# A gated feed-forward layer on one core: ten sums change from GpSimd to VectorE, and one unit more divides its S3 T3 product

## The chip, the cores and the metric

The kernel runs on one core of a Trainium2 chip. A core has a matrix engine (TensorE; PE in the profile, PEld for its weight loads), a vector engine (VectorE, DVE), an engine for functions (ScalarE, ACT), a general one (GpSimd, POOL), and a queue that starts DMAs (SyncE, SP). Each engine works through its own list of instructions in order and waits where one needs a result of another engine. The metric is the device time of one execution in microseconds; lower is better.

## The reference

The layer has 2048 tokens of width 1024 and an inner width of 3584, all in bfloat16:

```python
g = jnp.einsum("bsd,df->bsf", x, w_gate)      # 2048 x 1024 times 1024 x 3584
u = jnp.einsum("bsd,df->bsf", x, w_up)
h = gelu(g) * u                               # tanh form
return jnp.einsum("bsf,fd->bsd", h, w_down)   # 2048 x 3584 times 3584 x 1024
```

## The kernel before

**Products by seven instead of eight.** The kernel multiplies matrices as 2 x 2 blocks with Winograd's scheme: seven block products and some sums in place of eight products. On the weights' side the sums are called S1 to S4, on the side of x they are T1 to T4; a block that is only copied to another type is sa or tb. The sums are float32, so their matmuls read 128x512 float32 tiles.

**Tiling.** Tokens are worked in two passes p of 1024, each pass in two halves of 512 columns. The inner width is cut into 14 units of 256 columns (NU = 14), two blocks of 128 each, for w_gate and w_up (i = 0, 1). A block product (product) takes KH = 4 matmuls of 128x512, one per 128 rows of a half of K. For a unit and a pass the seven products are P1 (raw weights), S and G (raw, second half of K, for passes 0 and 1), P6 (S2 T2), P5 (S1 T1), and S4 Tb, SA T4 and S3 T3.

**Three stages.** First the units 0 to 2, one pass at a time (unit, over the list items; the last item is unit 0, pass 1). Then the joint units 3 to 13 (JOINT = 3), which take both passes together. Then the down projection (down).

**The second division.** In the joint units a product for gate and up and for both passes is itself a 2 x 2 block matrix: rows are gate and up, the inner index is the two halves of four K blocks, columns are the two passes. inner cuts it again by the same scheme: seven half products of two matmuls each, 14 matmuls, in place of four whole products of four, 16. Its left sums are quarter sums of S (half_sums, split_sums, on POOL); its right sums go over both passes. For these, split_b makes for each k of 0 and 1, from blocks b11, b12, b21 and b22 (rows: halves of K, columns: passes), n1 = b12 - b11, n2 = b22 - n1 and n4 = b21 - n2; split_b_rest makes n3 = b22 - b12 in place of b12, and so must come after everything that reads b12 as it was. The products named X (S4 Tb) and K (SA T4) are divided in all joint units. H (S3 T3) is divided from unit DIVIDED7 = 5 on; in units 3 and 4, H2, H3 and H4 are the whole products and the other H names do nothing.

**Where the T sums are made.** Those of Tb: split_b("tb") on POOL in the first stage, the rest in the last item's p4 (line 1117). Those of T4: there as well, split_b("t4") ahead of whole_p4 and split_b_rest("t4") behind it, all on POOL (pool, line 108). Some results go to a tile named w that more_room takes from the weights' pool. Those of T3: split_b3 in three parts, part 0 (three sums) at the end of unit DIVIDED7 - 1 (at @t4.1), parts 1 and 2 (three and two) in unit DIVIDED7 (at @s3), ahead of that unit's S3.

**What sets the order.** The order of SP, DVE, POOL, PE and ACT is that of the program (manual_schedule). In the joint units it is written out by hand as a list of names: SEQUENCE_FIRST for unit 3, SEQUENCE for the others. A capital with a number is a product on PE; a small name is an addition, copy or function on DVE or ACT; a name with @ calls side_work, which issues sums on POOL and DMAs; a name with - belongs to the unit before. Additions in PSUM's banks and products there wait for one another: so f0 and f1 are banks that S0 and S1 fill, c11a and c11b (DVE) read, and seeds (ACT) fill anew for G0 and G1; xz6 (ACT) copies the bank that X6 filled before X7 goes on adding to it. Most temporary tiles come from one pool of 58 slots (SLOTS).

Of the kernel before, what the change touches and what calls it, by code (L numbers as in the profile page):

```python
# [10 lines left out]
def kernel(  # L11
# [19 lines left out]
    ADD, SUB, MUL = ALU.add, ALU.subtract, ALU.mult  # L31
# [14 lines left out]
    NWARM = 7  # L46
    JOINT = 3
    AHEAD = {(0, -2): 2, (0, -1): 2, (0, 1): 1, (1, -2): 1}
    DIVIDED7 = 5
    STAY = range(11, 14)  # L50
    KEEPS = [(u, n) for u in range(5, NU) for n in range({7: 2, 9: 2, 11: 2, 13: 3}.get(u, 1))]
    H, Q, R2 = NJ // 2, N // 2, range(2)
# [52 lines left out]
    def dve(out, a, b, op):  # L105
        nc.vector.tensor_tensor(out=out, in0=a, in1=b, op=op)  # L106

    def pool(out, a, b, op):
        nc.gpsimd.tensor_tensor(out=out, in0=a, in1=b, op=op)  # L109
# [190 lines left out]
    def blocks(name, k):  # L300
        return [T[p][name][h + k] for h in (0, 2) for p in range(2)]

    def split_b(name):
        n = ns[name] = [[], [], [], []]
        for k in range(2):
            b11, b12, b21, b22 = blocks(name, k)
            n1, n2, n4 = [place_n() for _ in range(3)]
            pool(n1, b12, b11, SUB)
            pool(n2, b22, n1, SUB)
            pool(n4, b21, n2, SUB)  # L310
            for got, t in zip(n, (n1, n2, b12, n4)):
                got.append(t)

    def split_b_rest(name):
        for k in range(2):
            b11, b12, b21, b22 = blocks(name, k)
            pool(b12, b22, b12, SUB)

    def split_b3(part):
        n = ns.setdefault("t3", [[], [], [], []])  # L320
        for k in range(2):
            b11, b12, b21, b22 = [T[p]["t3"][h + k] for h in (0, 2) for p in range(2)]
            if part == k:
                n1, n2, n4 = [slot([P, N], f32r, "n") for _ in range(3)]
                pool(n1, b12, b11, SUB)
                pool(n2, b22, n1, SUB)
                pool(n4, b21, n2, SUB)
                for i, t in ((0, n1), (1, n2), (3, n4)):
                    n[i].append(t)
            if part == 2:  # L330
                pool(b12, b22, b12, SUB)
                n[2].append(b12)
# [22 lines left out]
    def joint_ops(u, E, F):  # L355
# [85 lines left out]

        if u < DIVIDED7:
            for name in ("H1", "H5", "H6", "H7", "e00", "e10", "e01", "y5", "e11", "e10y"):
# [471 lines left out]
    def more_room():  # L915
        extra = wpool.tile([P, KH, N], f32r, name="w")
        spots["n"] += [extra[:, k] for k in range(KH)]

    def place_n():
        return spots["n"].pop(0)  # L920
# [6 lines left out]
    items = [(1, 0), (2, 0), (2, 1), (1, 1), (0, 1)]  # L927
# [41 lines left out]
    def load_next(u):  # L969
        if u < NU:  # L970
            ws[u] = load_w(u, u % 2 == 1)
# [13 lines left out]
    def side_work(u, what):  # L985
        def made(kind, n):
            if (u, n) in keeps:
                kind(keeps[u, n])

        more = u + 1 < NU  # L990
        name, part = what[:2], int(what[3:]) if what[2:3] == "." else None
        if what == "start":
            if u == JOINT:
                load_next(u + 1)
            made(fetch_wd, 1)
        elif what == "keep":
            made(keep_whole, 0)
        elif what == "store":
            if more:
                made(store_made, 0)  # L1000
            made(fetch_wd, 2)
        elif what == "s3":
            if u == DIVIDED7:
                split_b3(1)
                split_b3(2)
            if u > JOINT:
                new_s(u, "s3")
        elif name == "tb":
            if u > JOINT:
                half_sums(u, name, part)  # L1010
        elif name == "t3":
            if u >= DIVIDED7:
                half_sums(u, name, part)
            if more and part == 1:
                made(keep_whole, 1)
            if not more and part == 0:
                made(store_made, 0)
        elif what == "t4.0" and not more:
            half_sums(u, name, 0)
            half_sums(u, name, 1)  # L1020
        elif what == "t4.1" and not more:
            for n in range(1, 3):
                made(keep_whole, n)
        elif name == "t4":
            half_sums(u, name, part)
            if u == JOINT and part == 0:
                fetch_next(u)
            if u == DIVIDED7 - 1 and part == 1:
                split_b3(0)
        elif name in ("s1", "s2", "s4"):  # L1030
            if more:
                new_s(u + 1, what)
        elif what == "late":
            made(store_made, 1)
            if u > JOINT:
                fetch_next(u)
        elif what == "end":
            load_next(u + 2)
        if not more:
            last_loads(what)  # L1040
# [27 lines left out]
    with tc.manual_schedule(engines={ENG.Activation}):  # L1068
        for n, (u, p) in enumerate(items):
            first = n == 0  # L1070
            def after_p5():
                at_p5(n)

            def aside(part):
                if first and part < 0:
                    rest_of_0(part + 2)
                if first and part == 0:
                    t.make("t4")
                for v in loads.get((n, part), ()):
                    ws[v] = load_w(v, True)  # L1080
                turn_some(AHEAD.get((n, part), 0))
                if (n, part) == (1, -2):
                    two_sums("t2", XL[:, KH:], "t1")
                    two_sums("t3", XL[:, KH:], XL[:, :KH])

            def mid():
                if "sa" not in ss[u]:
                    ss[u]["sa"] = sums_s(loaded(u), pool)["how"]["sa"](None)

            def ahead_of_p4():  # L1090
                if n == 0:
                    raw_of(2, 0, even, cc)()
                elif n == 1:
                    p1 = [raw_first(e, 1, loaded(v)) for e, v in ((Eb, 2), (D, 1))]
                    raw_second(K, 1, loaded(2))
                    finish_raw(2, 1, K, p1[0])

                    T[1]["tb"] = spots["tb"]
                    for k in range(KH):
                        nc.scalar.copy(out=spots["tb"][k], in_=XT[1, 1][KH + k])  # L1100
                    new_room(0, 1, *["t4"] * KH, *["n"] * 3)
                    two_sums("t4", xT[1][:, KH:], "t2")
                    new_s(0, "s1", "s2", "s3", "s4")

                    def second_half():
                        raw_second(K, 1, loaded(1))
                        finish_raw(1, 1, K, p1[1])

                    nxt["c11"] = second_half
                elif n == 3:  # L1110
                    raw_of(0, 1, Ea, D)()

            def behind_p4():
                if "c11" in nxt:
                    nxt.pop("c11")()

            def p4(c12):
                times(p, 2 * u, 1, gelu(c12[0]), c12[1])
                if n == len(items) - 1:
                    split_b_rest("tb")  # L1120
                    more_room()
                    split_b("t4")
                whole_p4(u, p, banks[0], ss[u], ahead_of_p4, behind_p4)
                if n == len(items) - 1:
                    split_b_rest("t4")

            if first:
                banks = odd, cc, dd
                late = lambda: add(cc, nxt["p1"])
            else:  # L1130
                banks = (Eb, D, K) if n == 3 else (Ea, K, D)
                late = None
            unit(u, p, banks, ss[u], late, after_p5, aside, mid, p4)
            ss[u].pop("sa")
            if n == 1:
                Ea, Eb, K, D = Eb, D, K, Ea
            elif n == 3:
                Ea, Eb, K, D = Ea, K, D, Eb

        E, F = [Eb, K], [D, Ea]  # L1140
        last = None
        for u in range(JOINT, NU):
            now = joint_ops(u, E, F)
            steps = SEQUENCE_FIRST if u == JOINT else SEQUENCE
            for name in steps:
                if name[0] == "@":
                    side_work(u, name[1:])
                elif name[0] != "-":
                    now[name]()
                elif last:  # L1150
                    last[name]()
            last = now
            E, F = F, E
        for name in SEQUENCE:
            if name[0] == "-":
                last[name]()
# [51 lines left out]
```

## Time and profile before

| | us |
|---|---|
| median of 3 runs | 526.37 (526.24 to 526.38) |
| the profiled execution | 526.39 |
| its span, first to last instruction | 524.6 |
| PE busy | 518.7 (99%) |
| DVE busy | 390.6 (74%) |
| POOL busy | 336.9 (64%) |
| ACT busy | 293.6 (56%) |

The granted TensorE clock is 1.000. Times in the profile's rows are counted from the span's start. A row of the timeline reads: start, length, engine, line, operation, tiles written and read, shapes, how many instructions are merged, and in brackets how long the engine had been idle and what ended that. Nearly all sums share a line (DVE 106, POOL 109, matmuls 127), so groups are told apart by the tiles. h, t, tb, n and w stand for the places of T sums and their parts, s for sums of the weights, p, u, v, xz and kz for copies and sums of results, o and h (bfloat16, written by DVE) for the layer's inner values on their way out.

### The profile page before, as it was taken

How to read it: one execution, taken by the hardware profiler on the slowest of the kernel's cores; microseconds unless marked ns; L12 is line 12 of the kernel's file. 1: busy time of each engine (PE TensorE's matmuls, PEld its weight loads, DVE VectorE, ACT ScalarE, POOL GpSimd, SP SyncE). 2: the span in 40 equal slices, each digit the busy share in tenths (PEclk: the TensorE clock that was granted, in tenths of full speed). 3: DMA queues.
4: the chain of work that ended last, by engine and by line, in shares of the span. 5: the costliest groups of instructions: out<-in, count | busy, mean ns of one | idle time of the engine just before them, and what ended most of it. 6: DMA issues, size and time to landing. Idle time of an engine off the chain costs nothing.

```text
span 524.6 us, 7866 instructions
## 1 busy us (share of the span) xinstructions
PE 518.7 (99%) x2356; PEld 368.0 (70%) x2389; DVE 390.6 (74%) x598; ACT 293.6 (56%) x542; POOL 336.9 (64%) x339
## 2 busy tenths in 40 slices
PE   9999999999999999999999999999999999999997
PEld 5576877767667676767677676754788885488887
DVE  2984553687888989897988889897789226967934
ACT  3556655676778687878787787851135602142430
POOL 1079999998999999999999999840000000000594
PEclk9999999999999999999999999999999999999999
DMA  9961323032625457373727444999976999993732
GB/s 252 213 166 52 89 84 111 32 109 92 191 81 181 123 180 230 112 239 111 233 92 231 163 159 159 343 374 415 385 259 212 394 398 353 392 327 101 238 133 71
DMA packets 102730, 105.91 MB, mean 202 GB/s; under 512 B 19360, under 2 KB 80800, under 8 KB 102688
## 3 DMA queue, kind: packets, MB, share of 16 engines
q1 hardware_dynamic: 102688, 105.41, 61.4%
q8 instruction: 19, 0.31, 0.3%
q14 instruction: 23, 0.19, 0.1%
HBM read 72.61 MB, written 29.62 MB: 195 GB/s over the span
## 4 chain that ended last, share of the span: by engine, by line
PE 98%; DMA 1%; issue 0%; SPq 0%; DVE 0%
PE bank L127 98%; DMA xn<-in_x_dram 1%; SPq L797 0%; PE bank L804 0%; DVE st L106 0%
## 5 line engine op out<-in xcount | busy, mean ns | idle before, releaser
L127 PE MATMUL bank<-h,s 128*128 128x512 f32 x500 | 132.6, 395 | 0.0
L109 POOL TENSOR_TENSOR q<-q 128x256 fp32r<-128x256 f32 x28 | 26.6, 984 | 144.4 <-DMA q<-td 143.8
L127 PEld LDWEIGHTS bank<-h,s 128*128 128x128 f32 x500 | 93.9, 188 | 21.1
L127 PE MATMUL bank<-xT,w 128*128 128x512 bf16 (+1 forms) x446 | 106.8, 376 | 1.5
L127 PEld LDWEIGHTS <-w 128*128 128x128 bf16 x504 | 45.4, 98 | 59.1 <-issue 11.9
L109 POOL TENSOR_TENSOR s<-w 128x512 fp32r<-128x512 bf16 (+1 forms) x76 | 77.8, 1040 | 10.4 <-DMA w<-in_w_gate_dram 10.3
L127 PE MATMUL bank<-t,s 128*128 128x512 f32 x276 | 76.5, 400 | 0.0
L127 PE MATMUL bank<-q 128*128 128x512 f32 x264 | 65.6, 390 | 0.0
L127 PEld LDWEIGHTS bank<-t,s 128*128 128x128 f32 x276 | 51.9, 188 | 12.1
L127 PEld LDWEIGHTS bank<-q 128*128 128x128 f32 x264 | 49.6, 188 | 10.4
L123 ACT COPY p<-bank 128x512 f32<-128x512 f32 x72 | 40.6, 589 | 28.9 <-PE bank L127 28.6
L106 DVE TENSOR_TENSOR q<-h,h 128x512 fp32r<-128x512 bf16 x56 | 38.3, 684 | 16.8 <-DMA h<-hd 16.8
L123 ACT COPY u<-bank 128x512 f32<-128x512 f32 x62 | 35.8, 589 | 21.1 <-PE bank L127 21.0
L109 POOL TENSOR_TENSOR s<-s,s 128x256 fp32r<-128x256 f32 x60 | 44.8, 769 | 1.6
L106 DVE TENSOR_TENSOR xz<-bank,xz 128x512 f32<-128x512 f32 x44 | 30.2, 691 | 18.2 <-PE bank L127 14.6
L127 PEld LDWEIGHTS <-h 128*128 128x128 bf16 x224 | 21.7, 98 | 26.5 <-issue 0.5
L109 POOL TENSOR_TENSOR s<-w,s 128x512 fp32r<-128x512 bf16 (+1 forms) x37 | 39.4, 1081 | 0.0
L109 POOL TENSOR_TENSOR s<-s,w 128x512 fp32r<-128x512 f32 (+1 forms) x37 | 37.3, 1024 | 0.9
L118 ACT CAST tb<-raw 128x512 fp32r<-128x512 bf16 x28 | 16.9, 632 | 36.0 <-DMA raw<-in_w_down_dram 26.5
L109 POOL TENSOR_TENSOR m<-raw,m 128x512 fp32r<-128x512 bf16 x28 | 34.5, 1234 | 2.2
L106 DVE TENSOR_TENSOR bank<-bank,u 128x512 f32<-128x512 f32 x49 | 33.7, 688 | 0.0
L106 DVE TENSOR_TENSOR v<-bank,v 128x512 f32<-128x512 f32 x44 | 29.2, 684 | 2.1 <-PE bank L127 1.7
(122 smaller groups left out, 911.7 us busy)
## 6 DMA issues: line engine op xcount, KB each, us to landing
raw<-in_w_down_dram SPq DMA_DIRECT2D x68, 256.0 KB, 4.0
q<-td SPq DMA_DIRECT2D x66, 256.0 KB, 5.4
td<-m SPq DMA_DIRECT2D x42, 256.0 KB, 2.8
hd<-o SPq DMA_DIRECT2D x80, 128.0 KB, 1.7
h<-hd SPq DMA_DIRECT2D x17, 512.0 KB, 6.9
hd<-h SPq DMA_DIRECT2D x30, 128.0 KB, 1.7
h<-hd SPq DMA_DIRECT2D x5, 768.0 KB, 9.0
out_dram<-st SPq DMA_DIRECT2D x30, 128.0 KB, 4.6
```

Source lines behind the costliest of these rows:

```text
L106: nc.vector.tensor_tensor(out=out, in0=a, in1=b, op=op)
L109: nc.gpsimd.tensor_tensor(out=out, in0=a, in1=b, op=op)
L118: nc.scalar.copy(out=t, in_=src)
L123: nc.scalar.copy(out=t, in_=ps)
L127: nc.tensor.matmul(ps, lhsT=lhs, rhs=rhs, start=start, stop=stop, skip_group_check=True)
```

## The change

Two things. The second division of S3 T3 begins in unit 4 and not in unit 5: DIVIDED7 is 4. With it, part 0 of split_b3 moves into unit 3, and parts 1 and 2 into unit 4; unit 4 makes the quarter sums of its S3 and the seeds (e00, e10, e01), the copy (y5) and the additions (e11, e10y) that join the half products.

And the T4 sums over both passes (six of split_b, two of split_b_rest) and the two of split_b_rest for Tb go from POOL to DVE, all ten in a row at the start of unit 3, behind the last item's last product and ahead of unit 3's own additions. The extra tile w is taken there too, behind the load of unit 4's weights.

```diff
-    DIVIDED7 = 5
+    DIVIDED7 = 4
...
-    def split_b(name):
+    def split_b(name, eng=pool):
...
-            pool(n1, b12, b11, SUB)
-            pool(n2, b22, n1, SUB)
-            pool(n4, b21, n2, SUB)
+            eng(n1, b12, b11, SUB)
+            eng(n2, b22, n1, SUB)
+            eng(n4, b21, n2, SUB)
...
     def split_b_rest(name):
...
-            pool(b12, b22, b12, SUB)
+            dve(b12, b22, b12, SUB)
...
         if what == "start":
             if u == JOINT:
                 load_next(u + 1)
+                split_b_rest("tb")
+                more_room()
+                split_b("t4", dve)
+                split_b_rest("t4")
             made(fetch_wd, 1)
...
             def p4(c12):
                 times(p, 2 * u, 1, gelu(c12[0]), c12[1])
-                if n == len(items) - 1:
-                    split_b_rest("tb")
-                    more_room()
-                    split_b("t4")
                 whole_p4(u, p, banks[0], ss[u], ahead_of_p4, behind_p4)
-                if n == len(items) - 1:
-                    split_b_rest("t4")
```

## The prediction

> **What bounds the kernel now.** I read the page first: busy shares, then the chain that ended last.
>
> ```profile
> span 524.6 us, 7866 instructions
> PE 518.7 (99%) x2356; PEld 368.0 (70%) x2389; DVE 390.6 (74%) x598; ACT 293.6 (56%) x542; POOL 336.9 (64%) x339
> ...
> PE 98%; DMA 1%; issue 0%; SPq 0%; DVE 0%
> ```
>
> PE is busy for 518.7 of 524.6 us and is 98% of the chain; no other engine holds the end. So a change counts only if it alters the number of matmuls or makes PE wait. Next the table by stretches, one unit to a row. I took the unit starts from the timeline of PE: each unit from 4 on opens with a row of bf16 matmuls bank<-xT,w, at 107.75, 132.10, 155.99 and 179.88 us; unit 3 begins at 83.50.
>
> ```profile
> 83.50:107.75 24.25, 24.13 (x107) 17.17 (x109) 10.89 (x18) 15.13 (x28) 23.86 (x23) 1.00 0.34 99
> 107.75:132.10 24.35, 24.25 (x108) 17.10 (x109) 21.13 (x32) 16.99 (x32) 22.42 (x24) 1.00 0.28 87
> 132.10:155.99 23.89, 23.79 (x105) 16.72 (x107) 20.20 (x32) 18.42 (x35) 23.42 (x25) 1.00 0.44 137
> 155.99:179.88 23.89, 23.78 (x105) 16.72 (x106) 21.12 (x34) 18.55 (x35) 23.27 (x25) 1.00 0.45 144
> ```
>
> The columns are length, then busy time and instructions of PE, weight loads, DVE, ACT, POOL, then the granted clock (1.00), DMA share and GB/s. Unit 4 is 0.46 us longer than units 5 and 6. By the written orders it has 108 matmuls, they have 106 (a few records are missing). The units that already divide S3 T3 repeat at 23.89 us, so PE never waits there. POOL is busy nearly all the time, DVE only 10.89 us in unit 3. Where DVE is idle in unit 3, and what POOL does meanwhile, the timelines of the two engines show:
>
> ```profile
> 82.92 1.52 DVE L106 TENSOR_TENSOR h<-g,bank 128x512 bf16<-128x512 f32 x2
> 94.02 0.69 DVE L106 TENSOR_TENSOR p<-bank,p 128x512 f32<-128x512 f32 x1 [9.58 <-PE bank L127]
> ```
> ```profile
> 85.40 2.52 POOL L109 TENSOR_TENSOR h<-h 128x512 fp32r<-128x512 f32 x2
> ...
> 95.83 2.56 POOL L109 TENSOR_TENSOR h<-h 128x512 fp32r<-128x512 f32 x2
> 98.34 0.69 POOL L109 TENSOR_TENSOR s<-w 128x256 fp32r<-128x256 bf16 x1
> ...
> 116.44 1.30 POOL L109 TENSOR_TENSOR n<-h,t 128x512 fp32r<-128x512 f32 x1
> ```
>
> The ten sums that change engine run on POOL from 85.40 to 98.34. DVE is empty from 84.44 to 94.02, when it takes unit 3's first sum (c11a).
>
> **Part 1, the division in unit 4.** Removed: four whole S3 T3 products of 4 matmuls, 16. Added: seven half products of 2, 14. The price is the difference of two rows: 24.35 - 23.89 = 0.46 us for two matmuls (0.23 each), all on PE and so all on the path. -0.46 us.
>
> What unit 4 gains in other work: three ACT seeds (e00, e10, e01) and an ACT copy (y5) at 0.59 each, 2.4 us; two more DVE adds (e11, e10y) at 0.69; four quarter sums of S3 on POOL, 0.74 each, 2.9 us. In unit 5 the same steps stand in the same order with ACT at 18.42 of 23.89 us and PE without a wait, and ACT has 7.4 us idle in unit 4. I cost them at nothing; without that cover the first late seed would hold PE by one copy, 0.59.
>
> On POOL three T3 sums (116.44 to 120.47: 4.0 us) move from unit 4 into unit 3, and five more (135.51 to 142.34 in unit 5: 6.8 us) into unit 4, ahead of S3's own sums. No DMA is issued by any step moved; SP keeps its order. The load of unit 4's weights is now allocated ahead of the extra tile, so the two can trade buffers; both old contents (units 0 and 1) were last read before 83.50, SP issued the load at 84.96 and it landed at 90.59, so no wait comes of it.
>
> **Part 2, ten sums from POOL to DVE.** POOL loses 98.34 - 85.40 = 12.9 us. On DVE such a sum with both inputs in SBUF takes 0.69 us and starts 0.60 after the one ahead when POOL is quiet. Ten make 6.0 us, with four steps that need the result just made (about 0.09 each) 6.4: from 84.44 to 90.9, inside the hole. But POOL isn't quiet, and the trace shows that the two hold each other up:
>
> ```profile
> 130.19 1.16 POOL L109 TENSOR_TENSOR m<-raw 128x512 fp32r<-128x512 bf16 x1 [1.30 <-DMA raw<-in_w_down_dram]
> 131.43 2.74 POOL L109 TENSOR_TENSOR m<-raw,m 128x512 fp32r<-128x512 bf16 x2
> ```
> ```profile
> 130.31 1.59 DVE L106 TENSOR_TENSOR o<-v,v 128x512 bf16<-128x512 f32 x1
> ```
> ```profile
> 490.55 7.53 POOL L109 TENSOR_TENSOR q<-q 128x256 fp32r<-128x256 f32 x1 [143.84 <-DMA q<-td]
> ```
>
> The DVE product begun at 130.31 ends at 131.90, 0.55 after POOL's running one ended (131.35), and POOL's next takes longer. At 490.55 a POOL sum that usually takes 0.74 takes 7.53: DVE issues such sums back to back from there to 497.47, and POOL gets nothing in between. So: whoever is running finishes; DVE keeps POOL out while its sums follow without a break; a DVE sum that waits for its predecessor lets POOL in for one.
>
> The Trainium skill, page "SBUF — State Buffer", section "SBUF: two separate sides", says the same of one instruction: the pair of ports that both engines use is locked for a whole instruction, and the other blocks. It doesn't say who wins between two instructions; the 7.53 us row does.
>
> The row on DVE by this: starts when POOL's op ends at 84.76; ten times 0.60; four breaks (n1 to n2, n2 to n4, twice), each giving POOL one sum of some 0.6 us. 84.76 + 6.0 + 4 x 0.6 = 93.2 us, 0.8 ahead of 94.02. Bounds: 90.9 with POOL quiet; 97.6 if POOL slips in at every step (ten DVE sums at 0.56, POOL's last unit-3 quarter, its four quarters of the weights, three T3 sums of 1.15 and one weight sum, 12.9 in all). I take 93.2, because the 7.53 row is the only one with many DVE sums in a row. Cost: nothing.
>
> What stands behind the row on DVE is c11a, and behind that ACT:
>
> ```profile
> 94.74 0.63 ACT L373 ACTIVATE p<-p 128x512 f32<-128x512 f32 x1 [0.98 <-DVE p L106]
> 95.80 0.59 ACT L123 COPY v<-bank 128x512 f32<-128x512 f32 x1 [0.42 <-PE bank L127]
> 96.66 0.59 ACT L123 COPY v<-bank 128x512 f32<-128x512 f32 x1 [0.28 <-PE bank L127]
> 97.14 0.59 ACT L123 COPY xz<-bank 128x512 f32<-128x512 f32 x1
> ```
>
> The copy at 97.14 empties the bank that X7 goes on filling. X7 stands behind 66 of unit 3's 108 matmuls: 83.50 + 66 x 24.25/108 = 98.3. The copy ends at 97.73, so 0.5 is spare, and the gaps of 0.42 and 0.28 ahead of it make 1.2. The row may end as late as 95.2 before PE notices.
>
> **POOL's new dates.** Its last unit-3 quarter ends at 87.1 instead of 85.4, the four T4 quarters at 93.4 (98.34 + 2.65 = 101.0 before), the three T3 sums at 97.4, unit 4's S1, S2, S4 (6.8 us) at 104.2, four Tb quarters with the usual collision at 107.5, five T3 sums at 114.3, S3 at 116.6, the first T3 quarters at 118.1. H1 is the first to need S3: 60 matmuls stand ahead of it, 107.75 + 60 x 23.89/106 = 121.3. Some 4.5 us spare. After that POOL has 6.8 us less in unit 5.
>
> **Sum.** -0.46 + 0 + 0 = -0.46. The profiled execution took 526.39 (span 524.6 and 1.8 around it); the median of the three runs is 526.37, 0.02 less. 526.37 - 0.46 = 525.91. A measurement of this kernel can tell about 0.2%, 1.05 us, from no change; this is 0.09%.
>
> **Rivals.** First, POOL slips in at every step of the row, and the change is slower. The row ends at 97.6, c11a is 3.6 late, and past the 1.2 to 1.4 us of slack PE stands at X7 for 2.2: 526.4 - 0.46 + 2.2 = 528.1. It decides from 95.2 on. For it: every single DVE product beside POOL had to wait (1.59 at 130.31). Against: 7.53 at 490.55. Chance 0.08.
>
> Second, POOL is no earlier for the move. Then the T4 quarters start at 98.34 as before, the three T3 sums put everything behind them 4.0 later and the five another 6.8: the first S3 sum ends at 112.2 + 10.8 = 123.0, H1 waits 1.8 and H5, whose quarter is ready at 124.9, another 0.3: 526.4 - 0.46 + 2.1 = 528.0. Against: the ten DVE sums hold POOL for at most 6.0 of the 12.9 it is rid of, and some 20 of 58 slots were free in unit 3 by the order of first and last uses, so slots don't hold it back. Chance 0.05. The Trainium skill's "Perfetto Trace Analysis", section "Optimizing Scalar/DVE Operations", warns of this: the two share a read port, so moving work between them might not help. By that rule it would be the 528.0; by the rows above POOL still gains some 7 us.
>
> Third, one of unit 4's new seeds or quarters comes late by a copy or so, up to 0.6 or 0.9, and gives back what the two matmuls brought: 526.0 to 526.9. For it: no row shows unit 4 with them. Against: unit 5 has them without a wait. Chance 0.06.
>
> Fourth, faster by over 1.05 us: PE would need waits to lose in units 3 to 5, and the table shows none. Chance 0.02.
>
> **Numbers.** The forecast has 0.79: 525.91. Within 0.2%: forecast and third rival, 0.85; slower 0.13; faster 0.02. The range takes the forecast with 0.3 below and the third rival above, 525.6 to 526.9; outside are 0.15.
>
> **What would show it.** Unit 4 at 23.89 us between the two bf16 rows, all later starts 0.46 earlier; the ten sums on DVE between 84.4 and 93.5 with four gaps; c11a still near 94.0; POOL's w<-t,h rows gone, three n<- sums near 94 to 97 and one POOL sum stretched to some 2.4 us. Wrong, if c11a starts after 95.2, if PE shows a gap over 0.3 before X7 in unit 3 or H1 to H4 in unit 4, or if unit 4 isn't 23.89.

## The result and the profile after

The kernel became slower: 528.21 us (median of 7, 527.76 to 528.50) against 526.75 for the kernel before on the same chips (median of 7, 526.24 to 527.07), a ratio of 1.0028 with an interval of 1.0017 to 1.0040. That is 1.46 us more, where 0.46 less was forecast. The profiled execution took 527.76, with a span of 526.0.

The head of the page, with the chain that ended last:

```profile
span 526.0 us, 7914 instructions
PE 520.2 (99%) x2387; PEld 367.6 (70%) x2387; DVE 402.9 (77%) x610; ACT 295.1 (56%) x546; POOL 331.5 (63%) x333
...
PE 96%; POOL 1%; issue 1%; DMA 1%; SPq 0%; DVE 0%; POOLq 0%
```

PE was 98% of the chain and is 96%; POOL has come into it. The table by stretches, for units 3, 4 and 5 (length, then busy time and instructions of PE, weight loads, DVE, ACT, POOL; clock, DMA share, GB/s):

```profile
83.33:109.59 26.26, 24.53 (x109) 17.07 (x109) 23.57 (x28) 14.77 (x28) 24.40 (x22) 1.00 0.31 86
109.59:133.49 23.90, 23.90 (x108) 16.72 (x107) 21.21 (x34) 18.88 (x36) 21.11 (x23) 1.00 0.30 89
133.49:157.38 23.89, 23.89 (x108) 16.72 (x107) 20.46 (x33) 18.39 (x35) 21.86 (x24) 1.00 0.46 143
```

An instruction that runs across the end of a row is counted in both rows: of unit 4's 108 matmuls, 106 begin in it. Unit 4 shrank from 24.35 to 23.90 as forecast. Unit 3 grew from 24.25 to 26.26, by 2.01. The sum, 2.01 - 0.45 = 1.56, less 0.17 because unit 3 happens to begin at 83.33 and not at 83.50 in this execution, is the 1.4 by which the span grew. Where unit 3 stands still, the timeline of PE says:

```profile
97.20 1.07 PE L127 MATMUL bank<-h,s 128*128 128x512 f32 x4
100.00 1.16 PE L127 MATMUL bank<-h,s 128*128 128x512 f32 x4 [1.73 <-POOL s L109]
```

PE is idle for 1.73 us ahead of X7; start to start the step takes 1.9 longer than the 0.23 it should, and the next 0.08. The releaser in brackets is the last event that the profile finds. What X7 needs is the bank that ACT's copy xz6 empties, and the timelines of DVE and ACT show why that is late:

```profile
84.18 2.02 DVE L106 TENSOR_TENSOR h<-h 128x512 fp32r<-128x512 f32 x2
86.13 1.15 DVE L106 TENSOR_TENSOR h<-h,t 128x512 fp32r<-128x512 f32 x1
87.32 1.05 DVE L106 TENSOR_TENSOR h<-h 128x512 fp32r<-128x512 f32 x1
88.40 1.05 DVE L106 TENSOR_TENSOR w<-t,h 128x512 fp32r<-128x512 f32 x1
89.37 1.17 DVE L106 TENSOR_TENSOR w<-h,t 128x512 fp32r<-128x512 f32 x1
90.57 1.67 DVE L106 TENSOR_TENSOR w<-h,w 128x512 fp32r<-128x512 f32 x1
92.27 1.66 DVE L106 TENSOR_TENSOR w<-t,w 128x512 fp32r<-128x512 f32 x1
93.85 3.34 DVE L106 TENSOR_TENSOR h<-h 128x512 fp32r<-128x512 f32 x2
97.11 0.68 DVE L106 TENSOR_TENSOR p<-bank,p 128x512 f32<-128x512 f32 x1
```
```profile
97.82 0.63 ACT L373 ACTIVATE p<-p 128x512 f32<-128x512 f32 x1 [4.24 <-DVE p L106]
98.36 1.05 ACT L123 COPY v<-bank 128x512 f32<-128x512 f32 x2
99.30 0.60 ACT L123 COPY xz<-bank 128x512 f32<-128x512 f32 x1
```

In place of 0.69 us, the first two sums take 0.89 and 1.21, the next four 1.05 to 1.17 and the last four 1.66 to 1.77. The row ends at 97.19; c11a follows at 97.11 (due 94.02 - 0.17 = 93.85), the function on ACT at 97.82, the two copies, and xz6 ends at 99.90. X7 starts at 100.00. POOL in the same stretch:

```profile
85.62 1.11 POOL L109 TENSOR_TENSOR s<-w 128x256 fp32r<-128x256 bf16 x1
86.81 1.01 POOL L109 TENSOR_TENSOR s<-s,w 128x256 fp32r<-128x256 f32 x1
...
89.95 1.74 POOL L109 TENSOR_TENSOR n<-h,t 128x512 fp32r<-128x512 f32 x1
91.77 1.61 POOL L109 TENSOR_TENSOR n<-h,n 128x512 fp32r<-128x512 f32 x1
```

A quarter sum of 0.68 takes 1.01 to 1.13, a T3 sum of 1.30 takes 1.61 to 1.74. The two engines take turns, one instruction each: DVE's second sum ends at 86.21, POOL's running one 0.52 later, DVE's third 0.55 after that. DVE's second and third sums need nothing from the one ahead of them, and POOL got in there as well. This is the prediction's first rival, nearly to the number: it had the row's end at 97.6, a wait of 2.2 and 528.1 us.

### The profile page after: what moved, and what is told of

Same layout as the page of the kernel before. It is cut to its first block, busy times and chain, and to the rows that moved or that the text cites. A ratio compares the mean times of both kernels' runs of the same rounds, so it can differ in the third digit from the quotient of the medians.

```text
span 526.0 us, 7914 instructions
## 1 busy us (share of the span) xinstructions
PE 520.2 (99%) x2387; PEld 367.6 (70%) x2387; DVE 402.9 (77%) x610; ACT 295.1 (56%) x546; POOL 331.5 (63%) x333
## 4 chain that ended last, share of the span: by engine, by line
PE 96%; POOL 1%; issue 1%; DMA 1%; SPq 0%; DVE 0%; POOLq 0%
PE bank L127 96%; POOL s L109 1%; DMA w<-in_w_up_dram 1%; POOL n L109 1%; SPq L797 0%; SPq L817 0%; DVE st L106 0%; POOLq L109 0%
## 5 line engine op out<-in xcount | busy, mean ns | idle before, releaser
L127 PE MATMUL bank<-xT,w 128*128 128x512 bf16 (+1 forms) x472 | 108.7, 377 | 0.1
L109 POOL TENSOR_TENSOR s<-w 128x512 fp32r<-128x512 bf16 (+1 forms) x76 | 81.3, 1084 | 10.4 <-DMA w<-in_w_gate_dram 10.3
L127 PE MATMUL bank<-t,s 128*128 128x512 f32 x272 | 75.4, 400 | 0.0
L109 POOL TENSOR_TENSOR s<-s,s 128x256 fp32r<-128x256 f32 x63 | 47.6, 777 | 1.7
```

Source lines behind the costliest of these rows:

```text
L127: nc.tensor.matmul(ps, lhsT=lhs, rhs=rhs, start=start, stop=stop, skip_group_check=True)
```

## The experiments

All changes are against the changed kernel, unless another is named.

**1. Part 1 alone.** The kernel before, with one line changed:

```diff
-    DIVIDED7 = 5
+    DIVIDED7 = 4
```

> Part 1 alone: S3 T3 is divided from unit 4, the ten T sums stay on POOL. Both theories (POOL and DVE take turns at every step of the row; the wait in unit 3 has another cause) agree that without sums on DVE unit 3 shows no wait at X7. What is open is whether unit 4 pays for itself: POOL gets 4.0 us of T3 sums in unit 3 and 6.8 us in unit 4 ahead of S3 and is rid of nothing, so that the first S3 sum ends near 123 and H1, due near 121.3, waits 1.8, H5 another 0.3: slower than before by 2.1 - 0.46 = 1.6 us. If POOL's dates have more room than I read, the 0.46 of the two matmuls is all: faster by 0.46.

Measured: 529.19 us (median of 4) against 526.64, ratio 1.0040 (1.0024 to 1.0055). Unit 3 takes its old 24.26, unit 4 27.81. PE and POOL around H1:

```profile
120.67 0.84 PE L127 MATMUL bank<-h,s 128*128 128x512 f32 x3
123.49 0.80 PE L127 MATMUL bank<-t,s 128*128 128x512 f32 x2 [1.97 <-POOL s L109]
```
```profile
119.78 2.54 POOL L109 TENSOR_TENSOR h<-h 128x512 fp32r<-128x512 f32 x2
122.26 2.29 POOL L109 TENSOR_TENSOR s<-w 128x512 fp32r<-128x512 bf16 x2
124.63 0.73 POOL L109 TENSOR_TENSOR s<-s 128x256 fp32r<-128x256 f32 x1
```

H1 waits 1.97 us for the first S3 sum, which begins at 122.26, as the prediction's second rival had it for a POOL that is no earlier (1.8). So in this order of POOL's sums the division doesn't pay unless POOL is rid of other work: the two matmuls bring 0.46, the sums that they ask of POOL cost more. The wait less the two matmuls is 1.5 us, and the medians differ by 2.55. The profiled execution, the slowest of the four at 530.01, holds a stretch at a lower clock besides, shown at the end. The other three, with a mean clock of 1.000, took 528.09 to 529.23; what the slower two of them lost beyond such a wait is not shown.

**2. Part 2 alone.**

```diff
-    DIVIDED7 = 4
+    DIVIDED7 = 5
```

> Part 2 alone: the ten sums on DVE at the start of unit 3, S3 T3 divided from unit 5 as before. Theory of turns: POOL has sums queued all through the row here too (the T4 quarters, then unit 4's S1 and S2), so the row still ends near 97, c11a starts there instead of 94.0, PE waits 1.7 to 1.9 us at X7, and the kernel is 1.9 us slower than before (no matmul is saved). If the wait came of part 1's earlier T3 sums, the row ends near 93 and the time is that of before, within 0.2 us.

Measured: 528.37 us (median of 5) against 526.64, ratio 1.0031 (1.0018 to 1.0043). Units 3 and 4:

```profile
84.20:110.12 25.92, 24.36 (x108) 17.03 (x109) 23.23 (x28) 14.80 (x28) 20.38 (x19) 1.00 0.31 91
110.12:134.46 24.34, 24.23 (x107) 17.09 (x109) 20.04 (x32) 16.78 (x32) 17.31 (x17) 1.00 0.28 88
```

Unit 3 takes 25.92 us, 1.67 over the kernel before, unit 4 its old 24.34; the row on DVE ends at 97.75 with unit 3's start at 84.20. PE is idle for 1.44 us ahead of X7, a little less than was expected. The loss in unit 3 is part 2's, and it comes with other sums in POOL's queue too. Together the parts cost less (1.46) than part 1 alone (2.55), since part 2 takes away part 1's wait; against part 2 alone (1.73) the intervals tell no difference.

**3. POOL waits for the row.** The whole change, and behind the ten sums a one-element copy on POOL that reads the last of them:

```diff
                 split_b("t4", dve)
                 split_b_rest("t4")
+                pool_behind(ns["t4"][2][1])
```

> The whole change, and POOL is made to wait in unit 3 for the last of the ten sums (a one-element copy on POOL that reads it), so that DVE has the row to itself. Theory of turns: the row takes ten times 0.60 and four steps of 0.09, and two turns of POOL at its start, and ends near 91.5; c11a stands at about 94.0 as before, PE doesn't wait, POOL's later dates are those of the prediction (T4 quarters done near 94, S3 near 117, ahead of H1 at 121): faster than before by 0.46 us, than the change by 1.9. If the wait of PE doesn't come from POOL's turns, the row still ends near 97 and the time stays that of the change, or POOL is late in unit 4 by its wait and H1 shows a gap.

Measured: 526.39 us (median of 11) against 526.64, ratio 0.9993 (0.9984 to 1.0002). The table and DVE's row:

```profile
83.88:108.13 24.25, 24.13 (x108) 17.16 (x109) 18.04 (x28) 15.12 (x28) 17.94 (x21) 1.00 0.34 97
108.13:132.02 23.89, 23.79 (x105) 16.72 (x107) 20.79 (x33) 18.91 (x36) 23.34 (x24) 1.00 0.26 84
```
```profile
84.73 2.08 DVE L106 TENSOR_TENSOR h<-h 128x512 fp32r<-128x512 f32 x2
86.74 0.68 DVE L106 TENSOR_TENSOR h<-h,t 128x512 fp32r<-128x512 f32 x1
...
90.84 1.28 DVE L106 TENSOR_TENSOR h<-h 128x512 fp32r<-128x512 f32 x2
94.39 0.69 DVE L106 TENSOR_TENSOR p<-bank,p 128x512 f32<-128x512 f32 x1 [2.27 <-ACT xz L123]
```

But for the first two sums, which still meet POOL, each takes 0.69 or less; the row ends at 92.12, c11a is on time, unit 3 takes 24.25 and unit 4 23.89. PE waits nowhere in units 3 and 4. That is the 0.46 of the forecast in the units, and it settles where the change's loss came from: the loss goes when POOL does nothing beside the row, from its third sum on.

**4. The same, once more**, for a narrower interval.

> The same kernel as the one in which POOL waits for the whole row, once more in five rounds, since 0.46 us is less than the first five rounds could tell. The units say -0.46 (24.03 and 23.89 for units 3 and 4 where the kernel before has 24.03 and 24.35). If that is all, the ratio lies at 0.9991 with an interval of some 0.0009 to each side; if the time before unit 3 (which moves by 0.5 and more between executions) were changed by the kernel and not by chance, the ratio is 1 or over, as often as not.

Measured: 526.34 us (median of 11) against 526.65, ratio 0.9993 (0.9983 to 1.0002). The 24.03 that was expected for unit 3 counts from the first matmul that the trace holds; from the unit's start, as in the tables here, it is 24.25. The medians of experiments 3 and 4 lie 0.25 and 0.31 below those of the kernel before, and the intervals just hold 1. The gain of the units is real in the trace, and at the edge of what times can tell: unit 3 begins anywhere from 83.33 to 84.20 us in the profiled executions shown so far, though no kernel changes anything ahead of it.

**5. What DVE reads.** The kernel of the change, its ten sums reading bfloat16 tiles of x (shortened):

```diff
-                split_b_rest("tb")
+                raw_x = lambda t, k: xT[k // 2][:, k]
+                split_b_rest("tb", raw_x)
                 more_room()
-                split_b("t4", dve)
-                split_b_rest("t4")
+                split_b("t4", dve, raw_x)
+                split_b_rest("t4", raw_x)
```

> The whole change, but the ten sums on DVE read bfloat16 tiles of x (the same shapes and places of output; the T4 sums and the last of Tb are not what the reference needs, so only times are read, and none of the ten reads another's result). This tells why POOL got no turn for 7.5 us at 490.55 and a turn at nearly every step in unit 3. If the type that DVE reads decides (both inputs bfloat16 there for two of three, float32 in unit 3), POOL is kept out here: the row ends near 91.3, one POOL sum is stretched to 5 us or more, PE has no gap, faster than before by 0.46. If it is not the type but that POOL had sums queued before DVE came, they take turns as in the change: the row ends near 97, gap of 1.9 at X7, slower than before by 1.4.

Measured: 527.87 us in one run. DVE's sums in rows of 4, 4 and 2:

```profile
84.20 4.21 DVE L106 TENSOR_TENSOR h<-xT,xT 128x512 fp32r<-128x512 bf16 x4
88.34 5.63 DVE L106 TENSOR_TENSOR w<-xT,xT 128x512 fp32r<-128x512 bf16 x4
93.89 3.33 DVE L106 TENSOR_TENSOR h<-xT,xT 128x512 fp32r<-128x512 bf16 x2
```

The same row, ending at 97.22, and the same gap ahead of X7 (1.9). Neither the type nor DVE's waits for its own results matter: here no sum needs another.

**6 and 7. POOL comes back in the middle.** As experiment 3, but POOL waits for the third sum only; in the second kernel the T4 sums stand in the order n1, n1, n2, n2, n4, n4, so that DVE's row has no break.

```diff
-                pool_behind(ns["t4"][2][1])
+                pool_behind(ns["t4"][0][0])
```

> As with POOL made to wait for the row on DVE, but POOL waits for the third of the ten sums only (the first n1 of T4), so that it comes back into a row that is running. Two theories on why POOL got no turn at 490.55 and one at nearly every step in unit 3. Holder theory: an engine that finds the other's instructions running without a break stays out until a break; then POOL gets in at each of the four steps at which DVE waits for its own result, and nowhere else: the row ends near 94, c11a is on time or 0.5 late, no gap on PE. Turns theory: from POOL's return on (about 87.5) they take turns, one each: seven DVE sums at 1.1, or 1.6 against POOL's T3 sums, the row ends near 95.5 to 96, c11a 1.5 to 2 late, PE waits 0 to 0.6 at X7. In neither is POOL late for unit 4: 23.9 us there.

> The same return of POOL at the third sum, and the T4 sums in an order in which none needs the result made just before it (n1, n1, n2, n2, n4, n4), so that the row on DVE has no break. Holder theory: POOL's first sum is held from about 87.5 to the row's end, 4 us or more in one row of the trace as the 7.5 at 490.55, and the row ends near 92, as with POOL quiet. Turns theory: as without the new order, the row ends near 95.5 to 96 and no POOL sum takes over 2 us. Unit 4 takes 23.9 us by both.

Measured: 526.28 and 526.41 us, one run each. The row ends at 95.70 and at 94.71. DVE and POOL of the second kernel:

```profile
86.80 1.28 DVE L106 TENSOR_TENSOR h<-h,t 128x512 fp32r<-128x512 f32 x2
88.00 1.77 DVE L106 TENSOR_TENSOR w<-h 128x512 fp32r<-128x512 f32 x2
89.69 2.24 DVE L106 TENSOR_TENSOR w<-t,w 128x512 fp32r<-128x512 f32 x2
```
```profile
87.54 0.58 POOL L198 COPY seen<-h 128x1 f32<-128x1 f32 x1 [1.21 <-DVE h L106]
88.08 1.14 POOL L109 TENSOR_TENSOR s<-w 128x256 fp32r<-128x256 bf16 x1
```

POOL comes back at 87.54 into DVE's unbroken row, and its copy ends at 88.13, 0.05 us after the DVE sum that ran. The holder theory falls: who runs first does not matter in unit 3, they take turns from there on. The second row ends before the 95.5 to 96 that was expected, as five of its sums were through before the turns began. PE loses 0.2 us ahead of X7 in the first kernel and nothing in the second.

**8, 9 and 10. Why POOL was kept out at 490.55.** The row on which the prediction rested shows the opposite, and it is in the changed kernel too: the same POOL sum takes 7.65 us there.

```profile
491.78 7.65 POOL L109 TENSOR_TENSOR q<-q 128x256 fp32r<-128x256 f32 x1 [143.66 <-DMA q<-td]
```

In nine profiles (the kernel before, the change and experiments 1 to 7) this sum takes 6.7 to 7.8 us and ends 0.60 us after DVE's last sum. Experiment 8 puts a one-element copy ahead of it on POOL (in the kernel of experiment 3):

```diff
         b1, b2 = q4[t], q4[H + t]
+        if t == 0:
+            pool_behind(b1)
```

> What is special at 490.55, where one POOL sum took 7.5 us beside DVE's row? The kernel in which POOL waits for the row in unit 3, and at the end, ahead of that POOL sum, a one-element copy on POOL that reads the same tile and waits for the same load. If it is that POOL has been idle for 144 us (its first instruction is held, whatever it is), the copy takes about 7 us and the sum behind it 0.74. If it is the form of the sum (two halves of one tile) or of DVE's sums there, the copy is quick (0.2 to 0.7) and the sum is held until DVE's row ends near 497.5, 0.60 behind its last. If both get in within a turn, it was the arrival of a lone instruction. Time as without the copy, 526.3.

Measured: 525.89 us, one run.

```profile
490.27 6.74 POOL L198 COPY seen<-q 128x1 f32<-128x1 f32 x1 [144.17 <-DMA q<-td]
496.97 1.56 POOL L109 TENSOR_TENSOR q<-q 128x256 fp32r<-128x256 f32 x2
```

The copy is held for 6.74 us and the sums behind it take their 0.74. It is POOL's first instruction there that is held, a copy as well as a sum. Experiment 9 gives POOL, in the kernel of experiment 7, an extra sum of the form of 490.55 as its first back in unit 3:

```diff
-                pool_behind(ns["t4"][0][0])
+                first = ns["t4"][0][0]
+                pool(slot([P, 2, Q], f32r, "s")[:, 0], first[:, Q:], first[:, :Q], SUB)
```

> The other side of the same question: in unit 3 POOL comes back at the third sum of a row without breaks, and its first instruction is now an extra sum of the same form as the one at 490.55 (the left half of a tile from its right half, 128x256 float32). If the form decides, it is held to the row's end, 4 us or more, and the row ends near 92. If not, it gets in within one turn (under 1.3 us) and the two alternate as they did behind the one-element copy: row ends near 95. Unit 4 at 23.9 us by both.

Measured: 525.98 us, one run. The sum takes 1.05 us and the two alternate, the row ending at 94.78: the form doesn't matter. Experiment 10 keeps POOL at work at the end (in the kernel of experiment 3): twelve extra sums from 477 on, their result unused.

```diff
+    def pool_busy(n):
+        extra = slot([P, N], f32r, "q")
+        for _ in range(n):
+            pool(extra, q73[6][0], q73[6][2], SUB)
+
+    at_tail(1, 44, pool_busy, 12)
```

> The last question on 490.55: does POOL's long idleness keep it out, or the row that DVE runs there? The kernel in which POOL waits for the row in unit 3, and at the end twelve extra sums on POOL (128x512 float32, their result unused) that begin when DVE has made what they read, near 477, in a pause of DVE, and are still running when DVE's row of sums begins at 484.7. If idleness decides, they take turns from 484.7 on as in unit 3: each DVE sum about 1.1 to 1.7 us, PE perhaps held at the end, 1 to 5 us slower than without. If DVE's row there keeps POOL out by itself, one POOL sum is held from about 485 to 497.5, some 12 us, and DVE's sums stay at 0.69.

Measured: 532.93 us, one run, 6.5 above the median of experiment 3 where 1 to 5 were expected. DVE's row at the end, the same instructions that kept POOL out before:

```profile
484.80 1.78 DVE L106 TENSOR_TENSOR q<-h,h 128x512 fp32r<-128x512 bf16 x1
486.50 1.78 DVE L106 TENSOR_TENSOR q<-raw 128x512 fp32r<-128x512 bf16 x1
488.20 1.77 DVE L106 TENSOR_TENSOR q<-h,q 128x512 fp32r<-128x512 bf16 x1
```

With POOL at work when the row begins, they take turns here too: DVE's sums take 1.78 in place of 0.69 beside the extra sums and 1.21 beside the usual ones of 0.74, and PE waits several times, at most 1.83 us. So it isn't DVE's sums there that keep POOL out by themselves. The 7.5 us belong to a POOL that comes back after 144 us without work, into a row that DVE had run without it for 7.7 us (from 482.80 in the kernel before). Which of the two decides is not separated: in experiment 9, where POOL wasn't held, both were short (1.29 us without work, two DVE sums). What holds POOL is not shown.

## Why the prediction was wrong

- **Part 1's price** was right: 24.35 to 23.90 in unit 4, on the path. So was the cover: the new seeds, copy and additions in unit 4 cost PE nothing, in the change and in experiment 3.
- **POOL's dates** were right where they mattered. S3 was done at 116.64 (116.6 was forecast), ahead of H1, but that the number fits so well is luck. The T4 quarters were done at 89.99 and not at 93.4, the T3 sums at 95.06 and not 97.4, because POOL got more turns than it was given. POOL was still 1.8 ahead behind the Tb quarters (105.72 against 107.5), and then stood for 1.39 us, until 107.11, for PE, which was 1.97 late itself: two misses that cancelled. The second rival's condition, that POOL gains nothing by the move, didn't hold: it began unit 4's S1 at 95.03, with three T3 sums ahead of it, where it had been 100.99 without them. The rule that moving work between these two might not help (the Trainium skill, page "Perfetto Trace Analysis", section "Optimizing Scalar/DVE Operations") hit the other engine: POOL was helped, DVE was hurt.
- **The row on DVE** is the step that failed: "DVE keeps POOL out while its sums follow without a break". POOL got a turn at almost every step, breaks or none, and the row took from 84.53, when POOL let it in, to 97.19, 12.7 us. The step's own worst bound, 12.9 us from 84.76 to 97.6, was the truth, and both of its signs of being wrong came: c11a behind 95.2 and a gap ahead of X7. I took the nearer-looking of two kinds of evidence, the one row with many DVE sums, and not the single products beside a POOL at work: of the 20 products o<-v,v in the joint units of the kernel before, 19 took 0.77 to 1.59 us in place of 0.68. At 130.31 POOL had its next sum queued, and DVE still got in between. The row at 490.55 was special for a reason that stands in its own brackets: [143.84 <-DMA q<-td], POOL had been idle. While the row runs in unit 3, POOL never is. The rule of the Trainium skill, page "SBUF — State Buffer", section "SBUF: two separate sides" (one instruction locks the pair, the other blocks), decides nothing between instructions; within one, the rows agree with it: POOL's sum and DVE's that ends 0.55 us behind it, again and again.
- **The slack behind the row** was right: 1.2 was read from ACT's gaps, up to 1.4 allowed. c11a came 3.26 late and PE stood for 1.97, so 1.3 was absorbed.
- **"It decides from 95.2 on"** agrees with experiments 6 and 7: with the row's end at 95.70 PE lost 0.2 us, with 94.71 nothing.
- **The rivals:** the first one came, with its place, its mechanism and nearly its price; its chance of 0.08 was far too low: the rows in which DVE got in between two POOL sums spoke for it, and one row, with an idle POOL, against it.

A version without the loss is experiment 3's: POOL held back until DVE has had its row. Its median is 1.8 us below the change's. Against the kernel before it is 0.46 us shorter in the trace of units 3 and 4, and 0.25 and 0.31 in the medians, which the times can't tell from no change.

## What to carry to other kernels

Before moving two-input sums from POOL to DVE, look at what POOL does in the same stretch: beside a busy POOL a DVE sum costs its own 0.55 us and a whole POOL instruction, together 1.1 to 1.8 us here, and an idle hole on DVE must be measured in that price. If POOL has slack of its own, a wait that keeps it quiet for the row can be worth more than the overlap. When one row contradicts several others, read its brackets and ask what is special about it before building a forecast on it.

## What the runs showed of the hardware

- Sums with both inputs in SBUF on DVE and sums on POOL alternate instruction by instruction when both have work: DVE 1.05 to 1.22 us beside POOL sums of 0.68 to 0.74, 1.5 to 1.8 beside sums of 1.15 to 1.3, whatever the type, the order and who was there first (experiments 5 to 7, 9 and 10).
- POOL's first instruction after 144 us without work was held for the whole rest of an unbroken row on DVE: 6.5 to 7.8 us for a sum in ten profiles, 6.74 for a copy of one element in another.
- A wait of PE can cost more than its length. In the profiled execution of experiment 1, the 1.97 us wait is followed by a stretch at half the granted clock (the row from 124.00; columns as in the tables above):

```profile
121.00:124.00 3.00, 1.03 (x5) 0.56 (x4) 1.18 (x2) 1.34 (x3) 3.00 (x4) 1.00 0.00 0
124.00:127.00 3.00, 2.78 (x7) 1.49 (x8) 0.79 (x2) 1.20 (x2) 2.84 (x5) 0.50 0.00 0
127.00:130.00 3.00, 3.00 (x13) 2.14 (x13) 2.63 (x5) 1.67 (x3) 2.92 (x5) 0.93 0.20 67
```

Unit 4 took 3.9 us more than 23.89 there, though PE's one long wait was 1.97. Experiment 10 has such a stretch too, behind a wait of 1.83 us that ended at 502.49 (one of 0.91 had ended at 498.52); from 503.50 to 505.00 the clock was 0.50:

```profile
500.00:505.00 5.00, 3.17 (x11) 2.04 (x9) 5.00 (x6) 0.39 (x1) 4.84 (x5) 0.84 0.39 115
505.00:510.00 5.00, 3.72 (x13) 2.38 (x12) 5.00 (x6) 0.67 (x2) 3.62 (x5) 0.81 0.74 236
```

The waits of 1.73 us in the change and 1.76 in experiment 5 left the clock at 1.00. The Trainium skill, page "TensorE: Matmul & The Clock Gate", section "Part 1: The HAM clock gate (the "warmup" mystery)", puts the step down to half speed behind an idle window of about 3.4 us; here the step down came behind waits of 1.97 and 1.83 us, once each, and what decides between these and the 1.76 is not shown.
